# 32x64 tiles for the last 15 blocks of a DFT, fp32r page transposes, and new places for loads, scatters and routing steps

## The chip, the cores and the metric

One core of a Trainium2 chip. The metric is device time in microseconds (us) from start to end of one execution, and the median over the runs is given. One further execution was run under the profiler. All rows come from that one. PE is the matrix engine (PEld its weight loads), DVE the vector engine, ACT the scalar engine, POOL GpSimd, SP the queue that issues most transfers.

## What is computed

Two layers, one behind the other. The first is a long convolution with a gate, for 4 sequences of 10048 positions and 128 channels:

```python
h_filt = (np.maximum(pos_emb @ w1, 0.0) @ w2) * window
y = irfft(rfft(x * v, n=2 * S) * rfft(h_filt, n=2 * S))[:, :S, :]
attn = x * y
```

The second is a mixture of experts on the 40192 rows of `attn`: each row picks one of 4 groups and one of the group's 4 experts by a maximum over logits, and gets `weight * (relu(row @ w1[g, e]) @ w2[g, e])`, with a weight that comes from two softmaxes.

## The kernel before

**Convolution.** A sequence is cut into 79 blocks of 128 positions. A DFT over the blocks (79 inputs, 79 complex outputs, 158 columns) is followed by one over positions (128 folded into two halves of 64), a product with the filter's spectrum, and the way back. The filter's own spectrum is made first, from a small network (`network`, line 534) and `filter` (586). Then come five rounds, b = 0 to 4 (loop at line 250). A round has two parts:

- The *pass* (loop at 262) walks over 22 units of channels: 20 of six and two of four. For batch b it runs the DFT over blocks of each unit (`dft_unit`, 408, two units at each even step, a *pair*, 11 in a pass). For batch b-1 it runs the way back over blocks: transposes (`turned`, 694: lines 704 and 707), `inverse_rest` (713, line 719) and `inverse_blocks` (728, line 740). Pass 0 has no batch to bring back, and the last pass has no DFT.
- The *middle* (loop at 294, 40 steps) runs the DFT over positions (line 506), the product with the spectrum (two multiplications on DVE, 672 and 675, two sums on POOL, 673 and 676) and the way back over positions (line 685). The way back of a step is issued four steps later (`LAG`), so PE has five steps of line 506 before its first 685.

In `dft_unit` the 79 blocks are split: 64 *main* blocks fill 64 rows of PE, and two channel halves and two folded halves give four 64x64 tiles (line 416, 158 columns each). The other 15 blocks of three channels stand together in 48 rows, with a weight table `fr` that is zero off its diagonal (line 423, 474 columns each). fp32 matmuls appear as two records each. The results leave two banks: `z` by ACT (and `zr` by ACT in pass 0, by DVE later, line 438).

**Routing.** Between, a generator is advanced by `next(routing)`. `chosen` (807, 22 steps) stores the rows of batch b-1 to memory, transposes them on PE (821), computes logits (829), turns them (846) and picks experts on DVE in three bursts (`choose`, 782). `ranked` (868) then counts and numbers the rows on DVE (880 to 922), and only then are 79 *scatters* a batch listed. A scatter is an indirect write by POOL of 128 rows to the page table `prow` (line 383), with rows loaded back by SP, four scatters a load (372), into four buffers. `self.scatter(n)` puts up to n of them into POOL's program at that place, and each waits for `self.pace`, the last copy that was emitted before it. In a pass the calls are 1 for each unit's DFT, and 1 (from j = 6 on 2) for each unit's way back. In a middle they are 1 at three of four steps. `next(routing)` runs at 25 of the 40 steps of a middle, twice behind it, and once for each unit of the next pass.

**Experts.** `moe` (1081) works through pages of 512, 384 or 256 rows of one expert. A page is loaded (`load`, 1288), transposed on PE in fp32 against `ident` (`turn`, line 1306, 320 transposes in all), split into a high and a low fp32r part (1313, 1314), and runs through two layers as three fp32r products each (1351 to 1353 and 1371 to 1373). Its result is transposed back in fp32 (1385), weighted (1392) and scattered (1397). Each engine runs its program in the written order.

Of the kernel before, what the change touches and what calls it, by code (L numbers as in the profile page):

```python
# [77 lines left out]
def make_consts():  # L78
# [14 lines left out]

    fr = np.zeros((2, KM, 2, GD, 2 * NB))
    for i in range(GD):
        fr[:, 16 * i : 16 * i + NB - KM, :, i] = fa[KM:].reshape(-1, 2, 2 * NB)
# [61 lines left out]
class Kernel:  # L158
# [62 lines left out]
    def conv(self, ctx, right):  # L221
# [7 lines left out]
        self.fm = cp.tile([128, 2, 2 * NB], F32, name="fm")  # L229
        self.fr = cp.tile([128, 2, GD, 2 * NB], F32, name="fr")  # L230

# [18 lines left out]
        for b in range(self.nbat + 1):  # L250
# [11 lines left out]
            for j, (d0, n) in enumerate(OUTS):  # L262
                if b > 0 and j % 2 == 0:
                    tts = self.turned(d0, min(2 * GI, D - d0))
                for i in range(j, j + 2) if not last and j % 2 == 0 else ():
                    self.run_ahead(b, i, made, folded)
                    self.scatter(1)
                    self.dft_unit(*folded[i])
                if b > 0:
                    if j % 2 == 0:  # L270
                        pos = self.inverse_rest(min(2 * GI, D - d0), tts)
                    self.inverse_blocks(b - 1, xy, d0, n, tts, pos[j % 2], j % 2)
                if not last:
# [18 lines left out]
            if not last:  # L292
                back = []
                for i, (k0, n) in enumerate(groups(NB, 2)):
# [112 lines left out]

    def dft_unit(self, b, eo, d0, n):

# [3 lines left out]
        for i in range(m):  # L413
            for h, hs in enumerate(HALVES):
                for ps, rs in zip(pss, HALVES):
# [3 lines left out]
                    if b and d0 == i == h == 0 and ps is pss[0]:  # L419
                        self.tc.keep_in_program_order(ins)  # L420
        for h, hs in enumerate(HALVES):
            for ps, rs in zip(pss, HALVES):
                nc.tensor.matmul(
                    ps[hs, :m].rearrange("p d k -> p (d k)"),
                    eo[rs, m, hs],
                    self.fr[rs, h, :m].rearrange("p d k -> p (d k)"),
                    start=False,
                    stop=True,
                )
        for r, ps in enumerate(pss):  # L430
            ds_ = slice(d0 + r * m, d0 + r * m + m)
# [102 lines left out]
    def network(self, ctx, eo):  # L534
# [11 lines left out]
        for j, m in groups(64, 4):  # L546
# [534 lines left out]
    def moe(self, ctx, right, routing):  # L1081
# [168 lines left out]
class Page:  # L1250
# [37 lines left out]
    def load(self, pool=None):  # L1288
        k, nc, pg = self.k, self.k.nc, self.k.pages
        self.xg = (pool or k.sp).tile([128, self.th, RW], F32, tag="xg", name="xg", bufs=1 if pool else XG)  # L1290
# [4 lines left out]
        ins = nc.sync.dma_start(self.xg, src.rearrange("(p h) c -> p h c", h=self.th))  # L1295
        k.tc.keep_in_program_order(ins)
# [4 lines left out]
    def turn(self):  # L1301

        k, nc = self.k, self.k.nc
        self.px = k.psx.tile([128, self.rows_], F32, tag="px", name="px")
        for h in range(self.th):
            k.fix(nc.tensor.transpose(self.px[:, h * 128 : h * 128 + 128], self.xg[:, h, 0:128], k.ident))  # L1306

    def rows(self):
# [8 lines left out]
        self.weight = k.sp.tile([128, self.th], F32, tag="wt", name="wt", bufs=4)  # L1317
        k.fix(nc.vector.tensor_copy(self.to, self.xg[:, :, 128]))
        k.fix(nc.vector.tensor_copy(self.weight, self.xg[:, :, 129]))

# [116 lines left out]
def layout(x, v, pos_emb, w1, w2, moe_w_group, moe_w_expert, moe_w1, moe_w2):  # L1437
# [44 lines left out]

    def unit(a, n):

        u = np.zeros((2, KM, n + 1, 2, 128), np.float32)
        for r in range(2):
            u[r, :, :n] = a[:KM, r * n : r * n + n]
            u[r, : 16 * n, n] = a[KM:, r * n : r * n + n].transpose(1, 0, 2, 3).reshape(16 * n, 2, 128)
        return u

    m = {
        "xv_in": np.concatenate([unit(xv[:, d0 : d0 + n], n // 2).ravel() for xv in xvs for d0, n in OUTS]),
        "x_out": c(
# [38 lines left out]
```

## Time and profile before

| | us |
|---|---|
| median of 3 runs | 1886.09 |
| lowest and highest run | 1885.25, 1890.03 |
| the profiled execution, its own time | 1890.19 |
| its span in the trace | 1888.4 |
| PE busy (share of the span) | 1796.0 (95%) |
| DVE, ACT, POOL busy | 1362.8, 1237.2, 977.0 |

The span is the stretch from first to last instruction; the own time lies 1.8 us above it. Stages by their first instructions: network and filter to 132 us, pass 0 to 180, middle 0 to 250, pass 1 to 333, middle 1 to 430, pass 2 to 517, middle 2 to 626, pass 3 to 714, middle 3 to 823, the last pass with the rest of the routing to about 940, experts to the end. A busy PE is not PE at its peak, so pace is read from the distance between starts.

### The profile page before, as it was taken

The page shows a single profiled execution, that of the slowest core. Times are in us where ns is not written, and L with a number is a line of the kernel's source. Part 1 is how long each engine was busy: PE and PEld are TensorE (multiplying, and loading weights), DVE is VectorE, ACT ScalarE, POOL GpSimd, SP SyncE. Part 2 cuts the span into 40 slices and gives each one's busy share as a digit, 9 for nine tenths or more (in the row PEclk, how much of TensorE's full clock was granted, in tenths as well). Part 3 has the DMA queues.
Part 4 walks back from the last instruction along what each step waited for, and adds up shares of the span by engine and source line. Part 5 has one row for each costly group of instructions (what it writes and reads, how often), then busy time and mean ns, then how long its engine had stood idle before and what let it go on. Part 6 is the DMA issues. An engine that isn't in the chain of part 4 may idle for free.

```text
span 1888.4 us, 43889 instructions
## 1 busy us (share of the span) xinstructions
PE 1796.0 (95%) x14662; PEld 1489.7 (79%) x14662; DVE 1362.8 (72%) x3068; ACT 1237.2 (66%) x2708; POOL 977.0 (52%) x1105
## 2 busy tenths in 40 slices
PE   7988999999989898988899999999999999999998
PEld 6866888777867686776688888888888888889998
DVE  5385777688758874873779877777777777777886
ACT  5474367436734574456677777777777777777886
POOL 3101820574899478967255556677666333333354
PEclk9999999999989998999899999999999999999999
DMA  4477975986889688865563333444443223222342
GB/s 135 141 281 261 306 242 167 315 265 222 264 294 307 212 275 284 304 210 188 179 210 113 112 111 122 156 135 135 123 132 117 90 89 91 89 87 84 97 130 90
DMA packets 201596, 338.18 MB, mean 179 GB/s; under 512 B 26904, under 2 KB 88445, under 8 KB 201360
## 3 DMA queue, kind: packets, MB, share of 16 engines
q1 hardware_dynamic: 170448, 274.87, 45.5%
q0 software_dynamic: 21408, 44.88, 6.7%
q10 hardware_dynamic: 9504, 15.54, 2.9%
q8 instruction: 118, 1.93, 0.4%
q14 instruction: 118, 0.97, 0.2%
HBM read 260.22 MB, written 75.53 MB: 178 GB/s over the span
## 4 chain that ended last, share of the span: by engine, by line
PE 53%; DVE 2%; ACT 1%; issue 1%; DMA 0%; SPq 0%; POOL 0%; ACTq 0%; DVEq 0%; POOLq 0%
PE py L1373 8%; PE py L1371 8%; PE ph L1351 8%; PE ph L1353 8%; PE py L1372 8%; PE ph L1352 8%; PE ptm L1385 2%; PE px L1306 2%; PE po L740 1%; PE po L719 1%; PE ptr L821 1%; DMA wf<-m_w 0%; PE pt L707 0%; PE plt L829 0%; ACT tt L709 0%
## 5 line engine op out<-in xcount | busy, mean ns | idle before, releaser
L1360 DVE SCALAR_TENSOR_TENSOR hl<-ph,hh 128x512 fp32r<-128x512 f32 (+1 forms) x656 | 441.6, 674 | 157.3 <-ACT hh L1359 152.2
L1397 POOL DMA_INDIRECT out<-os,to x320 | 318.4, 995 | 415.9 <-ACT os L1392 343.0
L1359 ACT ACTIVATE hh<-ph 128x512 fp32r<-128x512 f32 (+1 forms) x656 | 388.1, 592 | 170.4 <-PE ph L1353 140.1
L383 POOL DMA_INDIRECT prow<-stg,adr x316 | 331.5, 1049 | 133.3 <-issue 68.1
L1351 PE MATMUL ph<-xh,wh 128*128 128x512 f32 (+2 forms) x720 | 280.4, 389 | 6.0 <-ACT wh L1333 6.0
L1353 PE MATMUL ph<-xh,wl 128*128 128x512 f32 (+2 forms) x720 | 265.5, 369 | 1.6 <-DVE ep L1268 1.3
L1371 PE MATMUL py<-hh,wh 128*128 128x512 f32 (+2 forms) x720 | 264.5, 367 | 0.0
L1373 PE MATMUL py<-hh,wl 128*128 128x512 f32 (+2 forms) x720 | 264.4, 367 | 0.0
L1352 PE MATMUL ph<-xl,wh 128*128 128x512 f32 (+2 forms) x720 | 264.3, 367 | 0.0
L1372 PE MATMUL py<-hl,wh 128*128 128x512 f32 (+2 forms) x720 | 263.2, 366 | 0.0
L673 POOL TENSOR_TENSOR y<-t 128x256 f32<-128x256 f32 (+1 forms) x160 | 120.5, 753 | 210.1 <-DVE t L672 205.7
L692 ACT COPY z<-pbp 128x512 f32<-128x512 f32 x128 | 74.9, 585 | 190.0 <-PE pbp L685 190.0
L506 PE MATMUL psb<-z,bt 128*128 128x256 f32 x640 | 168.2, 391 | 28.9 <-issue 15.4
L685 PE MATMUL pbp<-y,bp 128*128 128x256 f32 x632 | 164.2, 383 | 3.4 <-POOL y L676 3.1
L672 DVE TENSOR_TENSOR t<-psb,ht 128x512 f32<-128x512 f32 (+1 forms) x160 | 108.8, 680 | 75.4 <-POOL y L676 21.8
L506 PEld LDWEIGHTS psb<-z,bt 128*128 128x128 f32 x640 | 119.3, 198 | 52.3 <-issue 27.5
L1353 PEld LDWEIGHTS ph<-xh,wl 128*128 128x128 f32 x720 | 136.3, 189 | 24.0 <-DVE ep L1268 1.8
L1351 PEld LDWEIGHTS ph<-xh,wh 128*128 128x128 f32 x720 | 136.6, 190 | 22.3 <-ACT wh L1333 6.7
L1372 PEld LDWEIGHTS py<-hl,wh 128*128 128x128 f32 x720 | 135.9, 189 | 21.8
L1373 PEld LDWEIGHTS py<-hh,wl 128*128 128x128 f32 x720 | 135.8, 189 | 21.8
L1371 PEld LDWEIGHTS py<-hh,wh 128*128 128x128 f32 x720 | 135.9, 189 | 21.3
L1352 PEld LDWEIGHTS ph<-xl,wh 128*128 128x128 f32 x720 | 137.1, 190 | 15.9
(230 smaller groups left out, 3480.9 us busy)
## 6 DMA issues: line engine op xcount, KB each, us to landing
ws<-m_w SPq DMA_DIRECT2D x180, 256.0 KB
xv<-xv_in SPq DMA_DIRECT2D x80, 512.0 KB
ht<-hspec SPq DMA_DIRECT2D x156, 256.0 KB
bt<-c_b SPq DMA_DIRECT2D x95, 256.0 KB
bp<-c_bp SPq DMA_DIRECT2D x76, 256.0 KB
xyd<-xy SPq DMA_DIRECT2D x76, 256.0 KB
stg<-xyd SPq DMA_DIRECT2D x76, 256.0 KB
xg<-prow SPq DMA_DIRECT2D x66, 260.0 KB
```

What stands on the lines that cost most here:

```text
L383: ins = self.nc.gpsimd.indirect_dma_start(self.d["prow"], bass.IndirectOffsetOnAxis(ap=u.adr[:, t : t + 1], axis=0), u.rows[:, t - u.t0], ...
L506: nc.tensor.matmul(ps[:, i].rearrange("p s d -> p d s"), bt[:, i], self.frequency(k0 + i, 1)[:, :, 0], start=True, stop=True,)
L685: nc.tensor.matmul(by_part[:, i], bp[:, i], y[:, i], start=True, stop=True,)
L1351: k.fix(nc.tensor.matmul(ph[:, j], wh, self.xh, start=True, stop=False))
L1352: k.fix(nc.tensor.matmul(ph[:, j], wh, self.xl, start=False, stop=False))
L1353: k.fix(nc.tensor.matmul(ph[:, j], wl, self.xh, start=False, stop=True))
L1359: k.fix(nc.scalar.activation(hh, ph, AF.Relu))
L1360: k.fix(nc.vector.scalar_tensor_tensor(hl, ph, 0.0, hh.bitcast(F32), ALU.max, ALU.subtract))
L1371: k.fix(nc.tensor.matmul(self.py, wh, hh, start=(c == 0), stop=False))
L1372: k.fix(nc.tensor.matmul(self.py, wh, hl, start=False, stop=False))
L1373: k.fix(nc.tensor.matmul(self.py, wl, hh, start=False, stop=(c == NC - 1)))
L1397: ins = k.nc.gpsimd.indirect_dma_start(k.d["out"], bass.IndirectOffsetOnAxis(ap=self.to[:, h : h + 1], axis=0), o, None, bounds_check=k.nt ...
```

## The change

1. `dft_unit` is split. `dft_main` issues the main matmuls of a unit. `dft_rest` then does the last 15 blocks of both units of a pair in 32x64 tiles: first two channels of each of the four banks (16 rows each, 316 columns), then the third channel alone (16 rows, 158 columns). `dft_leave` copies both units out behind that. The table `fr` and the input layout follow.
2. A pass puts 5 scatters into each pair (2 with the DFT, 1 and 2 with the way back) where there were 4 in the first three pairs and 6 in the others. A middle puts one at every second step, 20 in all, where there were 30.
3. In a middle `next(routing)` runs at each of the first 22 steps, and then at every third (6 more).
4. The page transposes take fp32r rows and an fp32r copy of the identity, made once by ACT.
5. The tables `fm` and `fr` are loaded by SP behind the network's other loads, and no longer by POOL near its front.

```diff
-    fr = np.zeros((2, KM, 2, GD, 2 * NB))
-    for i in range(GD):
+    fr = np.zeros((4, 32, 2, 2, 2 * NB))
+    for i in range(2):
         fr[:, 16 * i : 16 * i + NB - KM, :, i] = fa[KM:].reshape(-1, 2, 2 * NB)
...
-                for i in range(j, j + 2) if not last and j % 2 == 0 else ():
-                    self.run_ahead(b, i, made, folded)
-                    self.scatter(1)
-                    self.dft_unit(*folded[i])
+                if not last and j % 2 == 0:
+                    units = []
+                    for i in range(j, j + 2):
+                        self.run_ahead(b, i, made, folded)
+                        self.scatter(1)
+                        units.append(self.dft_main(*folded[i]))
+                    self.dft_rest(b, units)
...
                 if not last:
-                    self.scatter(1 + (j >= 6))
+                    self.scatter(1 + j % 2)
...
-                    self.scatter(i % 4 != 3, False)
-                    if i % 4 != 3 if i < 30 else i in (31, 33):
+                    self.scatter(i % 2, False)
+                    if i < CHOSEN or i % 3 == 0:
                         next(routing, None)
...
+    def dft_rest(self, b, units):
+        nc = self.nc
+        (one, _, m, low), (two, _, _, high) = units
+        banks = [(ps, slice(32 * g, 32 * g + 32)) for g, ps in enumerate(low + high)]
+        k = min(m, 2)
         for h, hs in enumerate(HALVES):
-            for ps, rs in zip(pss, HALVES):
+            for ps, rs in banks:
                 nc.tensor.matmul(
-                    ps[hs, :m].rearrange("p d k -> p (d k)"),
-                    eo[rs, m, hs],
-                    self.fr[rs, h, :m].rearrange("p d k -> p (d k)"),
+                    ps[hs, :k].rearrange("p d k -> p (d k)"),
+                    one[rs, m, hs],
+                    self.fr[rs, h, :k].rearrange("p d k -> p (d k)"),
                     start=False,
-                    stop=True,
+                    stop=m == k,
                 )
+        for h, hs in enumerate(HALVES) if m > k else ():
+            for ps, rs in banks:
+                rs = slice(rs.start, rs.start + 16)
+                nc.tensor.matmul(ps[hs, k], two[rs, m, hs], self.fr[rs, h, 0], start=False, stop=True)
+        for _, d0, m, pss in units:
+            self.dft_leave(b, d0, m, pss)
...
             if j == 16:
                 nc.sync.dma_start(self.fa.rearrange("p h k -> p (h k)"), d["c_fa"])
-                nc.gpsimd.dma_start(self.fm.rearrange("p h k -> p (h k)"), d["c_fm"])
-                nc.gpsimd.dma_start(self.fr.rearrange("p h c k -> p (h c k)"), d["c_fr"])
+            if j == 60:
+                nc.sync.dma_start(self.fm.rearrange("p h k -> p (h k)"), d["c_fm"])
+                nc.sync.dma_start(self.fr.rearrange("p h c k -> p (h c k)"), d["c_fr"])
...
+        self.identr = self.sp.tile([128, 128], F32R, tag="identr", name="identr", bufs=1)
+        nc.scalar.copy(self.identr, self.ident)
...
-        self.px = k.psx.tile([128, self.rows_], F32, tag="px", name="px")
+        px = k.psx.tile([128, self.rows_], F32R, tag="px", name="px")
         for h in range(self.th):
-            k.fix(nc.tensor.transpose(self.px[:, h * 128 : h * 128 + 128], self.xg[:, h, 0:128], k.ident))
+            k.fix(nc.tensor.transpose(px[:, h * 128 : h * 128 + 128], self.xg[:, h, 0:128], k.identr))
+        self.px = px.bitcast(F32)
```

`CHOSEN` is 22. `xg` becomes an fp32r tile that is loaded and read through fp32 views, and on the host the two units of a pair are packed together; both leave the transfers' sizes as they were.

## Rows read from the trace of the kernel before

**Rows 1.** Windows: PE, PEld, DVE, ACT, POOL busy (instructions), PEclk, DMA share, GB/s.
```profile
132.00:180.00 48.00, 42.61 (x694) 31.68 (x693) 29.35 (x72) 28.64 (x104) 0.00 (x0) 0.96 0.80 281
...
250.00:333.00 83.00, 82.89 (x1617) 67.41 (x1618) 58.70 (x145) 62.09 (x130) 0.59 (x2) 1.00 0.63 188
...
430.00:517.00 87.00, 84.73 (x1617) 68.27 (x1617) 65.55 (x163) 62.15 (x129) 51.13 (x54) 0.98 0.75 237
517.00:626.00 109.00, 95.66 (x579) 72.69 (x577) 79.42 (x159) 41.16 (x94) 99.35 (x126) 0.95 0.91 297
...
940.00:1884.00 944.00, 939.77 (x4862) 803.04 (x4860) 716.15 (x1527) 723.25 (x1490) 481.60 (x497) 1.00 0.37 117
```

**Rows 2.** Timeline of PE, one pair in pass 1: start, time, instruction, records.
```profile
290.62 1.04 PE L416 MATMUL psa<-fm,eo 64*64 64x158 f32 x24
291.48 0.97 PE L423 MATMUL psa<-fr,eo 64*64 64x474 f32 x8
292.27 0.98 PE L416 MATMUL psa<-fm,eo 64*64 64x158 f32 x24
293.08 0.97 PE L423 MATMUL psa<-fr,eo 64*64 64x474 f32 x8
293.87 0.98 PE L719 MATMUL po<-fi,tt 64*64 64x158 f32 x24
294.79 1.86 PE L740 MATMUL po<-fi,tt 128*64 128x79 f32 x48
296.58 0.55 PE L704 MATMUL pt<-ident,zr 128*128 128x128 f32 x3
...
298.37 0.50 PE L416 MATMUL psa<-fm,eo 64*64 64x158 f32 x8
```

**Rows 3.** The copies out of the DFT banks: ns min/median/max, whole run.
```profile
L438 ACT COPY z<-psa x176: 372/480/528, 137.1 to 712.4; 128x384 f32<-128x384 f32 x160, 128x256 f32<-128x256 f32 x16
```

**Rows 4.** Timeline, the start of middle 1 (first two rows) and middle 2.
```profile
332.88 2.00 PE L506 MATMUL psb<-z,bt 128*128 128x256 f32 x8
...
341.63 0.59 PE L685 MATMUL pbp<-y,bp 128*128 128x256 f32 x2
...
516.95 2.00 PE L506 MATMUL psb<-z,bt 128*128 128x256 f32 x8
...
519.01 0.98 POOL L383 DMA_INDIRECT prow<-stg,adr  x1 [0.30 <-issue]
...
530.45 0.74 POOL L673 TENSOR_TENSOR y<-t 128x256 f32<-128x256 f32 x1
...
533.85 1.91 PE L685 MATMUL pbp<-y,bp 128*128 128x256 f32 x4
```

**Rows 5.** Waits between 517 and 626 us: total, times, longest us.
```profile
PEld psb L506 <- issue: 8.3, 2, 8.1
```

**Rows 6.** Windows inside middle 1: columns as in rows 1.
```profile
333.00:388.00 55.00, 53.36 (x375) 41.07 (x376) 36.49 (x66) 24.60 (x59) 32.80 (x45) 1.00 0.96 321
400.00:430.00 30.00, 27.04 (x121) 21.21 (x120) 29.77 (x74) 10.60 (x21) 23.47 (x30) 1.00 0.76 247
```

**Rows 7.** Page transposes, two expert matmuls, and loads of L885 (timeline, lines).
```profile
L1306 PEld LDWEIGHTS px<-ident,xg x320: 138/140/225, 912.1 to 1866.5; 128*128 128x128 f32 x160
...
1044.59 0.44 PE px L1306 x4
...
1053.57 0.39 PE L1351 MATMUL ph<-xh,wh 128*128 128x512 f32 x1
1053.80 0.39 PE L1352 MATMUL ph<-xl,wh 128*128 128x512 f32 x1
...
417.66 0.30 PEld L885 LDWEIGHTS pc<-cnt,tri 128*128 128x128 f32 x2 [0.46 <-DVE cnt L880]
...
L885 PEld LDWEIGHTS pc<-cnt,tri 128*128 128x128 f32 x8 | 1.3, 188 | 2.5 <-DVE cnt L880 2.4
```

**Rows 8.** Timeline of ACT at the start.
```profile
9.05 0.46 ACT L524 CAST p<-pt 128x320 fp32r<-128x320 f32 x1 [3.24 <-DMA pt<-pos_t]
```

More of the change, by code (lines that the diff above doesn't have):

```diff
@@ L229, in conv @@
         self.fm = cp.tile([128, 2, 2 * NB], F32, name="fm")
-        self.fr = cp.tile([128, 2, GD, 2 * NB], F32, name="fr")
+        self.fr = cp.tile([128, 2, 2, 2 * NB], F32, name="fr")
         self.z = zp.tile([128, D, KM, 2], F32, name="z")
@@ L406, in clear, with dft_main @@
         return ins
-    def dft_unit(self, b, eo, d0, n):
+    def dft_main(self, b, eo, d0, n):
         nc, m = self.nc, n // 2
@@ L420, in dft_unit, with dft_leave @@
                         self.tc.keep_in_program_order(ins)
+        return eo, d0, m, pss
+    def dft_rest(self, b, units):
[3 more added lines that the diff above has]
+        k = min(m, 2)
         for h, hs in enumerate(HALVES):
-            for ps, rs in zip(pss, HALVES):
+            for ps, rs in banks:
                 nc.tensor.matmul(
-                    ps[hs, :m].rearrange("p d k -> p (d k)"),
-                    eo[rs, m, hs],
-                    self.fr[rs, h, :m].rearrange("p d k -> p (d k)"),
+                    ps[hs, :k].rearrange("p d k -> p (d k)"),
+                    one[rs, m, hs],
+                    self.fr[rs, h, :k].rearrange("p d k -> p (d k)"),
                     start=False,
-                    stop=True,
+                    stop=m == k,
                 )
+        for h, hs in enumerate(HALVES) if m > k else ():
[4 more added lines that the diff above has]
+            self.dft_leave(b, d0, m, pss)
+    def dft_leave(self, b, d0, m, pss):
+        nc = self.nc
         for r, ps in enumerate(pss):
@@ L1289, in load @@
         k, nc, pg = self.k, self.k.nc, self.k.pages
-        self.xg = (pool or k.sp).tile([128, self.th, RW], F32, tag="xg", name="xg", bufs=1 if pool else XG)
+        self.xg = (pool or k.sp).tile([128, self.th, RW], F32R, tag="xg", name="xg", bufs=1 if pool else XG)
         at = (pool or k.sp).tile([1, 1], I32, tag="at", name="at", bufs=1 if pool else 4)
@@ L1294, in load @@
         src = k.d["prow"][self.skip :][ds(row, self.rows_)]
-        ins = nc.sync.dma_start(self.xg, src.rearrange("(p h) c -> p h c", h=self.th))
+        ins = nc.sync.dma_start(self.xg.bitcast(F32), src.rearrange("(p h) c -> p h c", h=self.th))
         k.tc.keep_in_program_order(ins)
@@ L1317, in rows @@
         self.weight = k.sp.tile([128, self.th], F32, tag="wt", name="wt", bufs=4)
-        k.fix(nc.vector.tensor_copy(self.to, self.xg[:, :, 128]))
-        k.fix(nc.vector.tensor_copy(self.weight, self.xg[:, :, 129]))
+        k.fix(nc.vector.tensor_copy(self.to, self.xg[:, :, 128].bitcast(F32)))
+        k.fix(nc.vector.tensor_copy(self.weight, self.xg[:, :, 129].bitcast(F32)))
     def matrix(self, i, half, e):
@@ L1481, in layout, with both @@
     xvs = np.stack([xb[:, :, q], vb[:, :, q]]).transpose(1, 2, 4, 0, 3)
[L1483 to L1489, printed above, removed]
+    def both(xv, d0, n):
+        k, parts = n // 2, []
+        a = xv[:, d0 : d0 + 2 * n]
+        for second in range(2):
+            u = np.zeros((128, k + 1, 2, 128), np.float32)
+            for r in range(2):
+                o = second * n + r * k
+                u[64 * r : 64 * r + KM, :k] = a[:KM, o : o + k]
+            for g in range(4):
+                for i in range(2 * second, min(2 * second + 2, k)):
+                    o = 32 * g + 16 * (i % 2)
+                    u[o : o + NR - KM, k] = a[KM:, g * k + i]
+            parts.append(u.ravel())
+        return np.concatenate(parts)
     m = {
-        "xv_in": np.concatenate([unit(xv[:, d0 : d0 + n], n // 2).ravel() for xv in xvs for d0, n in OUTS]),
+        "xv_in": np.concatenate([both(xv, d0, n) for xv in xvs for d0, n in OUTS[::2]]),
         "x_out": c(
```

## The prediction

> **What bounds the kernel now.** I read the windows first, cut at the stages [rows 1]. PE is the thing to watch: it is full in pass 1 (82.89 of 83 us) and in the experts (939.77 of 944), so what is cut from PE's program there shortens the run. It isn't full in pass 0, where DMA moves 281 GB/s at a share of 0.80, nor in middle 2 (95.66 of 109), where POOL is busy for 99.35. A difference of 0.3% is about the smallest that a measurement of this kernel can tell from none.
>
> The timeline of one pair in pass 1 [rows 2] shows what fills PE. From 290.62 to 298.37 a pair takes 7.75 us: main matmuls 0.86 and 0.81, the last 15 blocks 0.79 twice, then 0.92, 1.79 and 1.79 for the way back and its transposes, with no gap.
>
> The starts of the middles [rows 4] show the other loss. Middle 1, without scatters, has its first way back 8.75 us after its first matmul (332.88 to 341.63). Middle 2 needs 16.9 (516.95 to 533.85), and middle 3 the same. The reason stands between: POOL is still sending the scatters of pass 2, and its first sum comes at 530.45. The waits agree: PE's loads of line 506 stood still once for 8.1 us [rows 5].
>
> **The change part by part.**
>
> *The last 15 blocks.* Today a unit has 8 records of 474 columns in 0.79 us [rows 2]. With the 24 records of 158 columns in 0.81 us, both come to 0.21 ns for a column. A transpose, which fills the whole array, takes 0.44 us for 4 x 128 columns [rows 7], 0.86 for a column, so four tiles run side by side at about 0.83. A pair costs 1.58. In the new form it has 16 records of 316 columns and 16 of 158. Eight tiles side by side would make that 16 x 316 x 0.83 / 8 = 0.53 and 0.26, together 0.79: a gain of 0.79. But no row shows records closer than 0.81 / 24 = 0.034 us. If that is a floor, the second part takes 0.54. Changing the tiles costs too: the 24 records of line 719, after which the tile shape changes, take 0.92 where the same shape takes 0.81, so 0.11 for a change, and a pair gets two more. That gives 0.53 + 0.54 + 0.22 = 1.29, a gain of 0.29. I take 0.42, nearer the lower end, since the floor is what rows show. In passes 1 to 3 there are 33 pairs: **-14 us** (-10 to -26).
> The Trainium skill (TensorE: Matmul & The Clock Gate, section "Wait — 56ns, not 53.3ns?") states that matmuls never start closer than about 25 ns. An estimate by that page would make the second part 0.40 and the gain 0.43; no row here is short enough to test it.
>
> The change adds a wait: a unit's copies now start when both units are done. Behind them on ACT stand the way back's copies. In passes 1 to 3, 4.5 us of PE work (0.92 + 1.79 + 1.79, rows 2) lie between the end of a pair and the next, and four copies of 0.48 [rows 3] fit. In pass 0 nothing lies between: the next pair waits for two banks, two copies of z and two of zr, about 1.4 us. PE's own need is 3.25 today and some 2.8 then, so 4.2 against the 48 / 11 = 4.4 us that DMA allows [rows 1]. The gain is hidden there, and the wait nearly so: **+1** (0 to +3).
>
> *Five scatters a pair.* A scatter takes POOL 0.98 + 0.30 us [rows 4]. Six take 7.7, all of a 7.75 us pair, so POOL never catches up after its late start in pass 2 (ranking ends at j = 1) and carries (530.45 - 516.95) / 1.28, some ten scatters, into the middle. Five take 6.4 against a new pair of 7.3. What is left at the end is the last pair's own, up to 6.4 us, and PE has 8.75 us of its own work before it needs POOL. So the stall goes: 16.9 - 8.75 = 8.2 in each of middles 2 and 3. I take 7.5 each, since the rest of a middle stays as it is (by the code it has 20 scatters for 25, and nine of them in its last 18 steps, where DVE binds): **-15** (0 to -17). The ten scatters that fall out go to the last pass, and from there into the experts, where POOL is idle for half of the time (481.60 of 944, rows 1). What is late next is DVE.
>
> *Choosing earlier, ranking thinner.* In middle 1 DVE is busy for 36.49 of the first 55 us, and for 29.77 of the 30 from 400 on [rows 6]. Pass 2 is then 87 long where pass 1 is 83 [rows 1], as ranking runs on into it. After the change the first 22 steps all carry choosing, PE is full and DVE has room, and ranking ends inside the middle. DVE has the same work left behind it, so the middle gets longer by nearly what the pass gets shorter. DMA is the next to bind: it ran at 321 GB/s and 0.96 in those 55 us, and a step with choosing moves 0.79 MB (spectrum, two tables, store) and half a scatter's 0.13, 2.7 us at that pace. For three rounds I take **-3**; the 4 us that passes 2 and 3 lose, as a gain or as a loss, bound it (-9 to +9 with the last pass).
>
> *fp32r transposes.* Four fp32 transposes take 0.44 us, 0.86 ns for a column; the fp32r matmuls of 512 columns start 0.23 us apart, 0.45 for a column [rows 7]. At that pace a transpose takes 57 ns in place of 110, and 320 would give 17 us. On the other side stands their weight load. Two loads of 128 columns in line 885 lie 0.30 - 0.188 = 0.11 us apart, which is the transposes' pace already; by that row nothing is won. The load of a transpose is shorter, though (140 against 188 ns, rows 7), and I take that as the nearest row and 75 ns as the price: 320 x 35 = **-11** (0 to -17). All of it counts, because PE is full there. The new copy of the identity is one short ACT instruction, hidden (ACT 723 of 944).
> The Trainium skill (TensorE: Matmul & The Clock Gate, "LDWEIGHTS (loading the stationary operand)") gives a load as columns / 1.2 ns, 107 ns for 128 whatever the type, which agrees with line 885 and not with the 140 ns of the transposes. By that rule this term is 0, and the sum 11 us higher.
>
> *Later loads.* At the start ACT waits 3.24 us for `pos_t` [rows 8], while POOL's two transfers (640 KB by their shapes) share the DMA engines. They move behind the last network load on SP, where nothing is needed from them before 132 us; the transfers of the filter's tables queue behind them and have tens of us to spare. **-2** (0 to -3.2).
>
> Sum: -14 + 1 - 15 - 3 - 11 - 2 = -44. From the profiled execution's 1890.2 that is 1846. That execution stands 4.1 above the median of the runs, so I forecast **1842 us**.
>
> **Rivals.**
> *A: the transposes stay load-bound.* For it line 885, against it the 140 ns load. 1842 + 11 = 1853.
> *B: the new tiles still go four at a time*, so that the split doesn't do what it says. The pair stays at 1.58 and pays its two tile changes (0.22 x 33 = 7). Against it: four work today without loss. 1842 + 14 + some 3 to 7, say 1861.
> *C: the middles' stall stays*, because scatters that wait for the last copies of a pass still reach POOL ahead of its sums, or the spectrum's transfers behind the reloads are late. Against it the 1.3 us that POOL gains for each pair. 1842 + 15 = 1857.
> *D, on the slower side: row tiles don't overlap at all*, and only the two column halves do. One after the other, the new records need 16 x (316 + 158) x 0.83 = 6.3 us for a pair; two at a time that is 3.16, with the changes 3.4 against 1.58, so +1.8 for each of 33 pairs, +59. The others give -30. The sum is 1886 + 29 = 1915. It decides below 2.5 at a time (6.3 / 2.5 = 1.58 + 30 / 33). Against it: the two row halves of today's 64x64 tiles overlap.
>
> **How the numbers follow.** I give the forecast 0.44, A 0.24, B 0.12, C 0.10, D 0.05, and 0.05 to several terms failing together, which ends within 0.3%. So faster 0.90, same 0.05, slower 0.05. The range takes in A, B and C, and at the other end the better ends of the tiles (12 more) and the transposes (6 more): 1824 to 1864.
>
> **What would show it.** Right: in pass 1 the last blocks of a pair take about 1.16 us on PE and the pair 7.3; the first way back in middles 2 and 3 comes some 9 us after the first matmul; four page transposes take 0.30; the first ACT wait is near zero; the middles end with DVE full and passes 2 and 3 begin without a gap. Wrong: rest blocks at 1.6 or more a pair, transposes at 0.44, a first POOL sum over 9 us into a middle, or PE waiting for copies between pairs of passes 1 to 3.

## The result, and the profile after

The changed kernel takes **1854.24 us** (median of 4 runs, 1850.58 to 1855.92), before in the same set 1885.67 (1884.48 to 1890.03). The ratio is **0.9827, 95% interval 0.9804 to 0.9850**: faster by 1.7%, 31.4 us. The forecast was 1842 with a range of 1824 to 1864, so sign and range held, with 12 us too much expected. The profiled execution took 1852.74 us against 1890.19, 37.5 less; before's lies 4 above its median, the changed kernel's 1.5 below.

The runs came from several chips. In this set and in the second set of experiments before takes 1884 to 1886 us; in the other three sets every kernel is longer (before 2079 to 2107), so only ratios to before of the same set are compared.

The stages after, cut where the first matmuls lie (these rows answer to [rows 1]):

```profile
core 0: us, PE busy (x) PEld busy (x) DVE busy (x) ACT busy (x) POOL busy (x), PEclk, DMA share, GB/s
244.00:322.00 78.00, 78.00 (x1754) 65.81 (x1755) 58.77 (x142) 60.29 (x127) 0.27 (x1) 1.00 0.65 197
...
421.00:501.00 80.00, 79.58 (x1774) 67.02 (x1776) 62.84 (x154) 61.17 (x129) 54.16 (x61) 1.00 0.86 269
501.00:607.00 106.00, 94.41 (x585) 71.04 (x581) 86.97 (x172) 40.72 (x94) 84.79 (x111) 1.00 0.88 290
607.00:688.00 81.00, 80.14 (x1772) 67.64 (x1774) 64.88 (x174) 61.12 (x129) 56.32 (x65) 0.98 0.86 270
```

Passes 1 to 3 are 78, 80 and 81 us long, with PE full in all three; before they were 83, 87 and 88. Middle 2 still isn't full on PE (94.41 of 106), and DVE's busy time in it grew from 79.42 to 86.97. Where the 37.5 us lie, from the starts of the same matmuls in both traces:

| stretch | before | after | difference |
|---|---|---|---|
| start to the filter's first matmul | 50.96 | 43.96 | -7.0 |
| filter, pass 0, middle 0 | 200.94 | 201.65 | +0.7 |
| pass 1 | 80.98 | 77.26 | -3.7 |
| middle 1 | 98.83 | 100.33 | +1.5 |
| pass 2 | 85.24 | 77.97 | -7.3 |
| middle 2 | 111.08 | 109.11 | -2.0 |
| pass 3 | 85.81 | 78.10 | -7.7 |
| middle 3 and last pass, to the first page transpose | 198.30 | 191.92 | -6.4 |
| experts | 976.21 | 970.58 | -5.6 |

Passes 1 to 3 and the experts, where PE is full, give 24 of the 37.5 us.

The timeline of PE over one pair of pass 1 answers to [rows 2] (start, length, engine, line, operation, count):

```profile
282.36 1.92 PE L419 MATMUL psa<-fm,eo 64*64 64x158 f32 x48
284.20 0.79 PE L434 MATMUL psa<-fr,eo 32*64 32x316 f32 x16
284.79 0.48 PE L444 MATMUL psa<-fr,eo 16*64 16x158 f32 x16
285.19 1.04 PE L741 MATMUL po<-fi,tt 64*64 64x158 f32 x24
286.16 1.86 PE L762 MATMUL po<-fi,tt 128*64 128x79 f32 x48
...
289.74 0.75 PE L419 MATMUL psa<-fm,eo 64*64 64x158 f32 x14
```

From 282.36 to 289.74 a pair takes 7.38 us, where it took 7.75. The last 15 blocks need 284.20 to 285.19, 0.99 where they needed 1.58. The neighbours pay: the main matmuls 1.84 for 1.67, the first part of the way back 0.97 for 0.92. A short window of the same timeline (284.78 to 284.84 us) shows that the records of eight tiles start together:

```profile
284.79 0.34 PE L444 MATMUL psa<-fr,eo 16*64 16x158 f32 x8
```

One by one, such eight start 5 to 9 ns apart, and the next eight follow 138 ns after the first (medians of pass 1). Four records of as many columns, on the four tiles of line 416 before, followed each other after 134 ns. So eight tiles do run side by side.

The start of middle 2, PE and POOL together (answers to [rows 4]):

```profile
501.17 2.00 PE L527 MATMUL psb<-z,bt 128*128 128x256 f32 x8
...
505.71 0.98 POOL L386 DMA_INDIRECT prow<-stg,adr  x1 [0.17 <-POOL stg L378]
...
506.72 0.73 POOL L695 TENSOR_TENSOR y<-t 128x256 f32<-128x256 f32 x1
...
509.46 0.69 DVE L694 TENSOR_TENSOR t<-psb,ht 128x512 f32<-128x512 f32 x1 [3.63 <-DMA ht<-hspec]
...
510.82 0.73 PEld L527 LDWEIGHTS psb<-z,bt 128*128 128x128 f32 x4 [1.43 <-issue]
...
511.79 1.02 PE L707 MATMUL pbp<-y,bp 128*128 128x256 f32 x4
```

POOL's first sum comes 5.6 us after the first matmul (before 13.5), the first way back after 10.6 (before 16.9). Middle 3 has the same two times. From here on the stretch from a middle's first matmul to its first way back is called its *head*. What this one has above the 9.2 us of middle 1 fits a wait for the spectrum: the first product of the third step waits 3.63 us on DVE for `ht`, and PE's loads for the fifth step stand for 1.43 us, until just after the third step's second product has ended.

### The profile page after: what moved, and what is told of

It is laid out like the page before. It is cut to its first block, busy times and chain, and to the rows that moved or that the text cites. A ratio compares the mean times of both kernels' runs of the same rounds, so it can differ in the third digit from the quotient of the medians.

```text
span 1850.9 us, 45142 instructions
## 1 busy us (share of the span) xinstructions
PE 1771.4 (96%) x15302; PEld 1474.7 (80%) x15302; DVE 1374.4 (74%) x3068; ACT 1232.2 (67%) x2709; POOL 960.8 (52%) x1103
## 4 chain that ended last, share of the span: by engine, by line
PE 80%; DVE 6%; DMA 3%; issue 3%; POOL 2%; ACT 1%; SPq 0%; DVEq 0%; POOLq 0%; ACTq 0%
PE ph L1376 8%; PE py L1398 8%; PE ph L1378 8%; PE py L1396 8%; PE py L1397 8%; PE ph L1377 8%; PE psb L527 6%; PE pbp L707 5%; PE psa L419 4%; PE po L762 4%; PE pt L729 3%; PE po L741 2%; PE ptr L843 2%; PE ptm L1410 2%; PE psa L434 1%
## 5 line engine op out<-in xcount | busy, mean ns | idle before, releaser
L386 POOL DMA_INDIRECT prow<-stg,adr x316 | 320.6, 1015 | 109.0 <-issue 57.3
```

The lines of the kernel that those rows point to most:

```text
L386: ins = self.nc.gpsimd.indirect_dma_start(self.d["prow"], bass.IndirectOffsetOnAxis(ap=u.adr[:, t : t + 1], axis=0), u.rows[:, t - u.t0], ...
```

## The experiments

**First set: one part alone on the kernel before** (before 2106.07 us). Each kernel is before with one part of the diff: the loads; the tiles (table, `dft_main`, `dft_rest`, `dft_leave`, input layout); the scatters; the routing steps.

e1_loads:

```diff
-                nc.gpsimd.dma_start(self.fm.rearrange("p h k -> p (h k)"), d["c_fm"])
-                nc.gpsimd.dma_start(self.fr.rearrange("p h c k -> p (h c k)"), d["c_fr"])
+            if j == 60:
+                nc.sync.dma_start(self.fm.rearrange("p h k -> p (h k)"), d["c_fm"])
+                nc.sync.dma_start(self.fr.rearrange("p h c k -> p (h c k)"), d["c_fr"])
```

e3_scatter:

```diff
-                    self.scatter(1 + (j >= 6))
+                    self.scatter(1 + j % 2)
...
-                    self.scatter(i % 4 != 3, False)
+                    self.scatter(i % 2, False)
```

e4_routing:

```diff
-                    if i % 4 != 3 if i < 30 else i in (31, 33):
+                    if i < CHOSEN or i % 3 == 0:
```

e2_tiles takes the first two hunks and those of the three functions from the diff of the change, and nothing else.

> The kernel before with the later loads alone. Theory of the later loads: the two tables no longer share the DMA engines with the first rows of the network, so the filter's first matmul comes at about 44 us instead of 51, everything behind it moves up unchanged, and the run is 6 to 7 us shorter. Rival, as the prediction had it: the wait of 3.2 us at the front goes and nothing more, -2 us, and the rest of the 7 us seen in the changed kernel is how that one execution began.

> The kernel before with the 32x64 tiles alone (scatters, routing steps, loads and page transposes as before). Theory of the sum: a pair takes 7.38 instead of 7.75 us, -0.37 for each of 33 pairs, -12 us in all, less about 1 in pass 0. Rival: POOL needs 7.7 us for the six scatters of a pair and can't follow a shorter pair, so passes 2 and 3 get shorter but the stalls at the front of middles 2 and 3 get longer by as much; then only pass 1 pays, -4 us, and the first way back of middle 2 comes 20 us after its first matmul instead of 17.

> The kernel before with the new scatter counts alone (five a pair, one at every second step of a middle). Theory: the stall at the front of middles 2 and 3 is POOL's backlog and goes with the sixth scatter, so the first way back comes 10 to 11 us after the first matmul instead of 17 and the run is 12 us shorter, with the middles' ends and the starts of passes 2 and 3 as before. Rival: it was the earlier end of ranking that let the scatters start earlier; then the counts alone leave over 14 us at the front of the middles and bring 4 us or less.

> The kernel before with the new places of the routing steps alone. Theory: DVE has the same work to do, so the middles get longer by what passes 2 and 3 get shorter (1.5 to 3 against 3 to 3.5 us), -1 to -4 us in all, and the stall at the front of middles 2 and 3 stays at 16 us or more. Rival: as ranking ends before the pass, its scatters start some 15 us earlier, POOL enters the middle without a backlog, and the stall goes by this part alone: -10 us or more.

| kernel | us | ratio to before | 95% interval |
|---|---|---|---|
| e1_loads | 2095.14 | 0.9938 | 0.9905 to 0.9971 |
| e2_tiles | 2137.13 | 1.0134 | 1.0092 to 1.0176 |
| e3_scatter | 2082.64 | 0.9895 | 0.9853 to 0.9937 |
| e4_routing | 2104.40 | 0.9989 | 0.9955 to 1.0022 |

The tiles alone made the kernel slower. The windows show where (e2_tiles, pass 1 and pass 2):

```profile
245.00:322.00 77.00, 77.00 (x1759) 64.87 (x1750) 58.87 (x143) 59.51 (x126) 0.00 (x0) 1.00 0.65 196
421.00:560.00 139.00, 119.52 (x1764) 88.19 (x1763) 66.34 (x160) 59.95 (x126) 56.42 (x62) 0.83 0.51 159
```

Pass 1 has no scatters and takes 77 us. Pass 2 runs the same matmuls beside the scatters and takes 139, with the granted clock at 0.83. The timeline of PE there:

```profile
479.02 0.72 PE L419 MATMUL psa<-fm,eo 64*64 64x158 f32 x4
480.01 0.45 PE L419 MATMUL psa<-fm,eo 64*64 64x158 f32 x3 [0.27 <-issue]
480.74 0.50 PE L419 MATMUL psa<-fm,eo 64*64 64x158 f32 x4 [0.28 <-issue]
481.50 0.50 PE L419 MATMUL psa<-fm,eo 64*64 64x158 f32 x3 [0.26 <-issue]
```

PE gets three or four records, then stands for 0.27 us with nothing that the profile shows to wait for. In this set pairs of passes 2 and 3 take 8 to 16 us, and pairs of pass 1 what they take elsewhere (7.75, or 7.38 with the new tiles). The first ten pairs of pass 2 take 10.2 us on the mean with the new scatter counts (e3_scatter), 11.5 and 11.1 with the old ones (e1_loads, e4_routing) and 13.1 with the old ones and the new tiles. So this set measures a limit that the first comparison doesn't have, and says little about PE's own work.

What it says of the expectations is this. e1_loads: the filter's first matmul comes at 43.72 us, against 51.13 and 49.60 in e3_scatter and e4_routing, which load as before; pass 1 starts at 244.0 us against 248.7 and 248.9. So 6 to 7 us are gained at the filter, as the theory had it, but "everything behind it moves up unchanged" fails: 4.7 us are left at pass 1. e3_scatter: the run is 23 us shorter instead of 12, and the heads of middles 2 and 3 are 10.1 and 8.6 us. But e1_loads, with the old scatters, has 9.3 and 9.8 here, so its heads don't decide between theory and rival. e4_routing: the time is the same within its interval; the heads are 19.0 and 9.5 us; the first two pairs of pass 2 take 8.0 and 8.1 us, where e3_scatter, with the old routing steps, has 10.9 and 8.9.

**Second set: the same questions where before takes 1883.67 us** (1880.15 to 1887.97, 17 runs). a0_after is the changed kernel, e2b_tiles the kernel of e2_tiles again. e5_transposes is before with the page transposes of the change (and `xg` as an fp32r tile):

```diff
+        self.identr = self.sp.tile([128, 128], F32R, tag="identr", name="identr", bufs=1)
+        nc.scalar.copy(self.identr, self.ident)
...
-            k.fix(nc.tensor.transpose(self.px[:, h * 128 : h * 128 + 128], self.xg[:, h, 0:128], k.ident))
+            k.fix(nc.tensor.transpose(px[:, h * 128 : h * 128 + 128], self.xg[:, h, 0:128], k.identr))
```

a3_no_scatter is the changed kernel with the scatters of before:

```diff
-                    self.scatter(1 + j % 2)
+                    self.scatter(1 + (j >= 6))
...
-                    self.scatter(i % 2, False)
+                    self.scatter(i % 4 != 3, False)
```

> The changed kernel itself, beside its own parts on one chip. On the chip of the first result it took 0.983 of before. On the chip of the four single parts (before 2106 us) the parts multiply to about 0.9938 x 1.0134 x 0.9895 x 0.9989 = 0.995 without the transposes. Theory (the parts add up, the chip decides how much): 0.983 where before takes about 1886 us, 0.99 to 1.00 where it takes about 2100. Rival (the parts need one another: shorter pairs pay only when the ways back have been fetched in time): 0.983 on either chip, with the passes 2 and 3 at 80 us.

> Before with the 32x64 tiles alone, once more, since on the chip of the first four runs passes 2 and 3 took 139 us where before's take 87 on the other chip, PE's records coming in bursts of four with pauses of 0.27 us that wait for nothing shown. Theory: the tiles shorten each of 33 pairs by 0.34 us, -11 us, and the longer records count only where PE is starved of instructions while POOL scatters: 0.994 on a chip where before takes about 1886 us, 1.013 again on one where it takes 2106. Rival (the tiles hurt by themselves because POOL has less time for the scatters of a pass and stalls the middles longer): at or above 1.000 on either chip, with way-back fronts of middles 2 and 3 longer than the 16.9 us of before.

> Before with the fp32r page transposes alone. Theory (the loads of 140 ns, not the matmuls, set the pace of a group of four; the changed kernel gains 0.06 us a group): -4 to -5 us, ratio 0.9975. The prediction's value of 35 ns for each of 320 transposes would be -11 us, ratio 0.994; no gain at all 1.000.

> The changed kernel with the scatters as before (three of four steps in the passes, one a step and then two in the middles). Theory: the stall at the head of middles 2 and 3 comes back at 6.3 us each and the passes lose nothing on PE: +13 us against the changed kernel (0.990 of before where that takes 1886). Rival (in shorter pairs POOL falls further behind, and the scatters it carries over lengthen the stall by the time that the pass is shorter, about 7 us a pass): +20 us or more, and heads of 20 us and over.

| kernel | us | ratio to before | 95% interval |
|---|---|---|---|
| a0_after | 1852.47 | 0.9829 | 0.9810 to 0.9847 |
| e2b_tiles | 1874.79 | 0.9956 | 0.9939 to 0.9973 |
| e5_transposes | 1879.76 | 0.9973 | 0.9961 to 0.9986 |
| a3_no_scatter | 1859.09 | 0.9862 | 0.9844 to 0.9880 |

*Tiles.* Here they gain 8.9 us. Full pairs take 7.37 or 7.38 us, but the first pairs of passes 2 and 3 take 11.9 and 12.1. The windows of e2b_tiles over the first of them and the rest of pass 2:

```profile
421.00:433.00 12.00, 8.47 (x171) 6.97 (x171) 11.63 (x31) 6.12 (x14) 0.00 (x0) 0.89 0.52 178
433.00:503.00 70.00, 70.00 (x1592) 59.02 (x1590) 52.85 (x127) 53.55 (x113) 48.66 (x53) 0.99 0.82 261
```

In its waits from 414 to 442 us (total, times, longest) stands

```profile
PEld pt L728 <- DVE zr L459: 3.8, 1, 3.8
```

DVE is busy for 11.63 of 12 us: the rest of the ranking stands in its program ahead of the copies that PE needs. The first three pairs of pass 2 took 27.5 us before (10.91, 8.84, 7.74) and take 27.1 here (11.93, 7.77, 7.38), so their shorter matmuls bring 0.4 us of 1.1; in pass 3 they bring nothing (28.1 and 28.2). The changed kernel's take 22.7. In these pairs the tiles need the new places of the routing steps. The routing steps don't need the tiles: without them they already shorten the first two pairs (e4_routing above). Of the 8.9 us about 3 lie ahead of pass 1, which starts at 243.95 us here and at 247.08 in e5_transposes. The rival was partly right as well: the heads of middles 2 and 3 grew, from 16.9 us to 17.8 and 17.9.

*Transposes.* By the medians 3.9 us, by the stretch from the first page transpose to the end 970.71 for 976.21, 5.5 us, 17 ns for each of 320. One group of four, PE and its loads, in the kernel before and then in the changed kernel (answers to [rows 7]):

```profile
1044.19 0.59 PEld L1306 LDWEIGHTS px<-ident,xg 128*128 128x128 f32 x4
1044.42 0.60 PE L1306 MATMUL px<-ident,xg 128*128 128x128 f32 x4
1044.75 0.19 PEld L1351 LDWEIGHTS ph<-xh,wh 128*128 128x128 f32 x1
1044.78 0.48 PE L1351 MATMUL ph<-xh,wh 128*128 128x512 f32 x1
...
1045.10 0.40 PE L1352 MATMUL ph<-xl,wh 128*128 128x512 f32 x1
```

```profile
1105.48 0.54 PEld L1330 LDWEIGHTS px<-identr,xg 128*128 128x128 f32 x4
1105.70 0.46 PE L1330 MATMUL px<-identr,xg 128*128 128x128 f32 x4
1105.97 0.19 PEld L1376 LDWEIGHTS ph<-xh,wh 128*128 128x128 f32 x1
1106.01 0.46 PE L1376 MATMUL ph<-xh,wh 128*128 128x512 f32 x1
...
1106.30 0.40 PE L1377 MATMUL ph<-xl,wh 128*128 128x512 f32 x1
```

The next matmul starts 0.31 us after the group's first, where it took 0.36 (77 and 90 ns for each). The next load starts 0.49 us after the first, where it took 0.56 (122 and 140 ns for each), though a load's recorded length is 140 ns in both. And the matmul behind the group is followed after 0.29 us, in place of the 0.23 that such matmuls take in a row. Loads lie further apart than matmuls in both kernels, and the 17 ns are what their pace gained. This fits the theory that they set the pace of the group; no run changes the loads alone.

*Scatters.* Without this part the changed kernel takes 6.6 us more, half of what the theory said, although the heads of middles 2 and 3 came back in full (a3_no_scatter, middle 2):

```profile
500.64 2.00 PE L527 MATMUL psb<-z,bt 128*128 128x256 f32 x8
...
515.01 0.74 POOL L695 TENSOR_TENSOR y<-t 128x256 f32<-128x256 f32 x1
...
518.43 1.06 PE L707 MATMUL pbp<-y,bp 128*128 128x256 f32 x2
```

A head of 17.8 us against 10.6 is 7.2 a middle, yet the middle (to the next pass's first matmul) is 112.3 against 109.1 us, 3.2. (The expectation's parenthesis has passes and middles the wrong way round; the diff above is what ran.) The rest is given back near the end. From the start of the middle, the first product of step 32 begins on DVE at 92.2 us in a3_no_scatter and at 83.9 after, that of step 36 at 100.3 and 95.2: of 8.3 us, 5.1 are left four steps on. After the change DVE, the third busy time in this row of the windows, is full there:

```profile
585.00:606.00 21.00, 15.61 (x65) 11.45 (x65) 21.00 (x40) 5.66 (x10) 18.33 (x25) 1.00 0.80 245
```

The timelines of DVE and POOL, first after, then a3_no_scatter:

```profile
588.37 1.54 DVE L930 TENSOR_TENSOR oh<-oh,c 128x4 f32<-128x4 f32 x1
588.47 0.74 POOL L698 TENSOR_TENSOR y<-t 128x256 f32<-128x256 f32 x1
589.15 0.73 POOL L695 TENSOR_TENSOR y<-t 128x256 f32<-128x256 f32 x1
...
594.59 1.80 DVE L933 TENSOR_TENSOR f<-f,oh 128x316 f32<-128x316 f32 x1
594.64 0.72 POOL L695 TENSOR_TENSOR y<-t 128x256 f32<-128x256 f32 x1
595.33 0.72 POOL L698 TENSOR_TENSOR y<-t 128x256 f32<-128x256 f32 x1
```

```profile
595.53 0.15 DVE L930 TENSOR_TENSOR oh<-oh,c 128x4 f32<-128x4 f32 x1
...
596.20 0.56 DVE L933 TENSOR_TENSOR f<-f,oh 128x316 f32<-128x316 f32 x1
```

The same ranking instructions take 1.54 and 1.80 us where they took 0.15 and 0.56: they last as long as two sums of POOL behind each other. With a scatter at every second step POOL is late by a scatter and runs its sums without a gap; in a3_no_scatter the scatters of the middle have run out by 584.86, its last one. These two are the largest such differences. Over the whole middle the instructions of DVE that both traces have take 3.9 us more after the change, some of them less. The products of line 694, with one input in PSUM, take about 0.68 us beside a sum of POOL and without one. The Trainium skill (SBUF — State Buffer, section "SBUF: two separate sides") says that DVE and GpSimd share a pair of ports under an exclusive lock, which a DVE operation with two SBUF inputs needs against a GpSimd operation that reads SBUF. The ranking's 1.54 for 0.15 us agrees with that, and so do the products. A run with the scatters outside the ranking's steps, which would test it, was not made.

**Third set: the changed kernel less one part, and one variant** (before 2106.97 us).

a4_no_routing has before's condition for the routing steps:

```diff
-                    if i < CHOSEN or i % 3 == 0:
+                    if i % 4 != 3 if i < 30 else i in (31, 33):
```

a1_no_loads has the diff of e1_loads the other way round. v1_fewer_at_end:

```diff
-                        self.scatter(1)
+                        self.scatter(1 if j < 20 else 0)
...
-                    self.scatter(1 + j % 2)
+                    self.scatter(1 + j % 2 if j < 20 else 0)
```

> The changed kernel with choosing and ranking placed as before. With the tiles alone the first pair of passes 2 and 3 took 11.9 and 12.1 us and the second 7.8 and 8.1, where the changed kernel has 8.0, 8.2 and 7.3. Theory (ranking that runs on into a pass keeps DVE from the first pairs, and the middle gives back less than a microsecond): first pairs near 12 us again, about +4 us a round in the passes, +7 to +10 us in all, ratio 0.987 to 0.988 of before. Rival (the work only changes places, as the run of this part alone suggests, 0.9989): first pairs near 12 us, but the middles shorter by the same, within 3 us of the changed kernel, 0.983 to 0.9845.

> The changed kernel with the filter's two tables issued early by POOL as before. The filter's first matmul came at 51.0 us before, at 44.0 after, and at 46.1 with the tiles alone, which load a table smaller by 162 KB. Theory (what counts is how much the two early transfers move, so the smaller table gave most of the gain): first matmul of the filter near 46, +2 to +3 us against the changed kernel, ratio 0.9842. Rival (the place of the transfers gives all of the 7 us, and 46.1 was chance): near 51, +7 us, ratio 0.9867.

> The changed kernel without scatters in the last pair of a pass; the five that fall out go later. At the head of middle 2 five scatters still stand before POOL's first sum (5.6 us after the first matmul; 2.6 in middle 1), and the first way back comes at 10.5 us where middle 1 has 9.1. Theory (POOL still holds the head): first sum at 2.6 us, first way back near 9.2, -2.6 us in all, ratio 0.9815. Rival (the spectrum's transfers hold it: DVE waited for them for 3.4 and 2.5 us behind the fourth unit, with the DMA engines at a share of 1.0): first sum at 2.6, first way back still at 10 or later, no gain, ratio 0.983.

| kernel | us | ratio to before | 95% interval |
|---|---|---|---|
| a4_no_routing | 2102.02 | 0.9969 | 0.9938 to 0.9999 |
| a1_no_loads | 2127.94 | 1.0106 | 1.0062 to 1.0151 |
| v1_fewer_at_end | 2115.49 | 1.0044 | 1.0013 to 1.0076 |

Passes 2 and 3 took 121 to 127 us again, and the changed kernel itself isn't in this set, so the times don't decide, and the stages must. a4_no_routing was the shortest of the three, 13 us below v1_fewer_at_end, and why is open. *Loads:* the filter's first matmul, in e2b_tiles (second set), a1_no_loads and v1_fewer_at_end:

```profile
46.10 0.49 PE L473 MATMUL psa<-fa,eoh 80*64 80x158 f32 x4 [0.46 <-ACT eoh L605]
```
```profile
47.63 0.49 PE L473 MATMUL psa<-fa,eoh 80*64 80x158 f32 x4 [0.46 <-ACT eoh L605]
```
```profile
43.80 0.49 PE L473 MATMUL psa<-fa,eoh 80*64 80x158 f32 x4 [0.46 <-ACT eoh L606]
```

With neither it comes at 49.6 to 51.1 us (before, e5_transposes, e3_scatter, e4_routing). The smaller table alone brings it to 44.8 to 47.6 (the first is e2_tiles), the later place alone to 43.7 (e1_loads), both to 43.1 to 44.0. So the theory holds in part: the smaller table removes 2 to 6 of the 7 us, the later place nearly all, and together they bring little more than the later place alone.

*Head:* in v1_fewer_at_end the first sum comes 2.55 us into middle 2 and the first way back 9.12, as in middle 1 (timeline of PE, POOL and DVE).

```profile
545.93 2.00 PE L527 MATMUL psb<-z,bt 128*128 128x256 f32 x8
...
548.48 0.90 POOL L695 TENSOR_TENSOR y<-t 128x256 f32<-128x256 f32 x1 [5.24 <-DVE t L694]
...
551.96 0.69 DVE L694 TENSOR_TENSOR t<-psb,ht 128x512 f32<-128x512 f32 x1 [1.37 <-DMA ht<-hspec]
...
555.05 1.02 PE L707 MATMUL pbp<-y,bp 128*128 128x256 f32 x4
...
556.41 0.69 DVE L694 TENSOR_TENSOR t<-psb,ht 128x512 f32<-128x512 f32 x1 [3.17 <-DMA ht<-hspec]
```

The numbers are those of the theory, but this doesn't decide between it and the rival. The spectrum too came earlier: the third step's first product starts 6.0 us into the middle after a wait of 1.37, where the changed kernel has 8.3 and 3.63, and the long wait of 3.17 lies behind the first way back. And in this set the kernels that keep the five scatters have short heads as well: 9.3 and 9.1 us in a4_no_routing, 9.5 and 10.0 in a1_no_loads. In the changed kernel's own trace the times speak for the rival's cause: PE stands until the products that waited for the spectrum are done. Whether POOL would hold the head without that wait stays open. Whether the five scatters cost as much elsewhere can't be read from 2115 us.

**Fourth set: the routing steps once more** (before 2079.24 us). The edit is that of a4_no_routing.

> The changed kernel with choosing and ranking placed as before, once more, since the first time before took 2107 us and pairs in passes 2 and 3 took 10 to 15 us whatever their content. Where before takes about 1885 us: theory (ranking that runs on into a pass keeps DVE from the first two pairs, some 4 us a pass, and the middle gives back under 1): first pairs of passes 2 and 3 near 12 us against 8.0 and 9.4, +7 to +10 us against the changed kernel, 1859 to 1863, ratio 0.987 to 0.988. Rival (the work only changes places): within 3 us of the changed kernel, 0.983 to 0.9845. Where before takes about 2106: first pairs near 11.3 again and about 0.997.

It took 2076.06 us, 0.9982 (0.9949 to 1.0016), and belongs to the second case of the expectation. The first pairs of passes 2 and 3 were 11.1 and 11.3 us (11.3 and 11.2 in a4_no_routing, 8.0 and 9.3 in v1_fewer_at_end), so the place of the gain is the expected one. Its size where before takes 1884 us was not measured directly.

## Why the prediction was right, and where its steps were off

The forecast was right in sign and range since PE sets the end in passes 1 to 3 and in the experts, and what was cut there counted. That the sum came so near is luck in part: tiles, scatters and transposes were set too high, loads and routing steps too low. The sum of -44 stands against -37.5 in the profiled executions. The kernels of the second set split their 31.2 us of medians: tiles -8.9 (1883.67 to 1874.79); transposes, loads and routing steps together -15.7 (to 1859.09); scatters -6.6 (to 1852.47). Of the 15.7, the experts' stretch gives 5.3 to the transposes (975.52 to 970.23). Loads and routing steps share the other 10.4, and no run here parts them. By the filter's start (46.10 to 43.74) 2.4 would go to the loads and 8.0 to the routing steps. But in these two executions pass 1 starts no earlier (243.95 and 245.03 us), so the routing steps' share may be all of it, 8 to 10 us.

- **Tiles, -14.** The pair was right, 7.38 for 7.33, but by luck, since two errors cancel. The floor of 34 ns for a record was none: it is a mean over tiles that run side by side, and single records start 5 to 9 ns apart. The second part needs two waves of 0.138 us, the 0.26 of eight tiles and not 0.54. The Trainium skill's floor of about 25 ns from start to start (TensorE: Matmul & The Clock Gate, section "Wait — 56ns, not 53.3ns?") doesn't hold for these records either; that 16 of them in 0.40 us make 25 ns each is chance. The changes of the tiles, on the other side, cost more than 0.22. The neighbours take 0.17 + 0.05 longer, and the new rows take 0.99 us where four waves at the pace of 0.138 for 158 columns make 0.83. Measured, the whole term is -8.9, some 3 of it ahead of pass 1, where the step had no gain. What it missed besides is DVE, which takes most of the gain of the first three pairs of passes 2 and 3 away while ranking runs there.
- **Pass 0, +1.** From the filter's start to pass 1 the change is +0.7, less than that stretch varies (196.9 in e5_transposes, which changes nothing there). Pass 0 itself takes 46.3 to 47.6 us in the five kernels with the old tiles and 47.6 to 50.5 in the nine with the new ones, 2.6 more on the mean. So the added wait isn't nearly hidden there, but stays inside the 0 to +3.
- **Scatters, -15.** The step that failed is "since the rest of a middle stays as it is". The head lost 6.3 us against 7.5 expected, and 4 of the 7.2 us that the scatters' places make at the head were given back where scatters now share the last steps with ranking. The prediction named those nine scatters and DVE as the binding engine there, and put no price on it. (Its 25 scatters of before should read 30; middle 2 sends 26 where it sent 35, with those carried over.) Measured: -6.6 in all.
- **Choosing and ranking, -3 (-9 to +9).** Mis-sized: -8 to -10 by the difference above, at or beyond the lower bound of -9. First pairs fell from 11.9 and 12.1 us to 8.0 and 9.1 (a3_no_scatter), and middle 2 grew by 0.8 (111.5 to 112.3). DVE time moved from a pass, where PE waited for it, to a middle that mostly had room.
- **fp32r transposes, -11.** Mis-sized: 17 ns each, not 35. The 0.44 us of [rows 7] is a stretch of the chain that ended last; on the timeline the next matmul comes 0.36 us after the group's first, and 0.31 after the change. Rival A is borne out in part: the loads lie further apart than the matmuls, but their pace is not fixed, and 5.3 to 5.5 us are gained (3.9 by the medians of e5_transposes). The Trainium skill's rule (TensorE: Matmul & The Clock Gate, section "LDWEIGHTS (loading the stationary operand)") gives 107 ns for a load of 128 columns, and by it nothing is won. The measured pace in a group is 140 ns before and 122 after, and the measurement decides.
- **Later loads, -2.** -7.0 from the start to the filter, the bound of 3.2 too low there. By e1_loads the later place alone gives that, and 4.7 us of it are left at pass 1. The ACT wait of [rows 8] isn't the whole cause. ACT's waits for `pos_t` fell only from 4.5 us in all to 3.3 (e1_loads 2.0), and where the other microseconds come from isn't shown. The longest of them is now 1.45 us (timeline of ACT, after):

```profile
7.76 0.46 ACT L545 CAST p<-pt 128x320 fp32r<-128x320 f32 x1 [1.45 <-DMA pt<-pos_t]
```

The two tables don't go behind the network's other loads, as the list of changes has it: SP issues them at 4.99 and 7.24 us, between those loads. Rivals B and D fall by the 0.99 us of the last blocks, C by the head of 10.6, although its late spectrum fits what that head has too much. The median of 1854 is next to A's 1853, but for other reasons too: by the medians of the second set scatters brought 8 us less than the sum has, transposes 6 and tiles with pass 0 4, and loads and routing steps together 5 more.

## What to carry to other kernels

When one engine is relieved, look at what the next one does in the same microseconds: the tiles shortened the matmuls of every pair, and the pairs in which DVE was still ranking gained next to nothing until ranking was moved. A stall removed at the head of a stage is worth only what survives to its end; compare the start of the same step late in the stage, not only the head. A mean over records that run side by side is no floor for one of them; look at single starts first. Scatters may be better placed in steps where DVE has room than in the ranking's; that version was not run.

## What the runs showed of the hardware

Each set of experiments ran on a chip of its own. In three of the four, passes with scatters were 110 to 139 us long, where they take 78 to 86 elsewhere, while the pass without scatters was equal to 0.01 us a pair. The experts, which scatter too, took 1101 to 1135 us there in place of 970 to 976, the largest part of the difference. Engines then stood without a shown cause: PE in bursts of three or four records, POOL up to 8.1 us ahead of a scatter (e2_tiles, pass 3). e2_tiles is the same program as e2b_tiles, whose pass 2 has this row:

```profile
421.00:503.00 82.00, 78.47 (x1759) 66.00 (x1757) 64.48 (x157) 59.66 (x126) 48.66 (x53) 0.98 0.78 249
```

82 us and 249 GB/s here, 139 us and 159 GB/s in e2_tiles. Whether it is the chip that differs, or something else of that hour, isn't shown either. Slow supply of PE's instructions beside the scatters would look like this, but no run tested it, and it stays open. The trace gives it no support so far: the larger of the two DMA queues for instructions moved the same 13 packets in pass 2 of both, and they were busy for the same time (0.6% of 139 us and 1.0% of 82), so a packet took no longer. It decides what a change is worth: on those chips the tiles alone cost 1.3%, and a kernel that differs from the changed one only in the last pair of each pass was 0.4% slower than before, where the changed kernel is 1.7% faster on the others. The changed kernel itself wasn't run there, so the two expectations of a0_after, which both have 0.983 where it ran, aren't told apart.

The pauses go with a lower clock. In pass 2 of e2_tiles the granted clock was 0.83 on the mean. It went to and fro between its two levels, 1.2 and 2.4 GHz: it fell after bursts and pauses like those shown, and rose again. Where it was at the lower level (0.50 in the row below), the 48 records of the way back (line 761), which started without a gap, took 3.43 us, where they take 1.86 in the pair shown above:

```profile
472.30:475.80 3.50, 3.50 (x50) 3.31 (x50) 0.69 (x3) 1.28 (x3) 0.12 (x1) 0.50 0.29 80
```
